# Decoding weights through PSUM, softmax scales moved, and a new order for the prologue

## The chip, the core and the metric

The kernel runs on one core of one Trainium2 chip. A core has five engines that work side by side, each through its own queue in order: TensorE (PE; its weight loads are shown as PEld), VectorE (DVE), ScalarE (ACT), GpSimd (POOL) and SyncE (SP, which here only starts DMAs). They pass work on by semaphores. Tiles lie in SBUF or in PSUM banks of 128 x 512 words, of which this part of the kernel uses eight; TensorE's results go to PSUM, and in this kernel only VectorE and ScalarE read it. [...] The metric is the device time of one execution in microseconds; less is better.

## The reference

```python
q_d = q.reshape(B, H, Sd, 4, D).mean(axis=3)       # also k_d, v_d; B, H, S, D = 4, 8, 576, 64
out_d = sm_attn(q_d, k_d, v_d)                     # softmax(q k^T / 8) v over the pooled sequence
out_up = np.repeat(out_d, 4, axis=2)
mask = np.abs(pos[:, None] - pos[None, :]) < 4     # local attention: 7 keys for each query
scores = np.where(mask, q @ k^T / 8, -1e9)
out_local = softmax(scores) @ v
x = (out_up + out_local) -> 2304 tokens x 512
h = x @ w_in; g = relu(h) ** 2; x = g @ w_out      # d_ff 2048
return ((x @ w_a) * (x @ w_b)) @ w_out2            # d_ff 1536
```

All inputs are fp32, but the host hands the weights over as 64-bit words, and the kernel makes fp32 from the two 32-bit halves itself.

## The kernel before, in words

The tokens are worked in nine tiles of 256. For the first feed-forward network each weight tile (32 of them: 16 of `w_in`, 16 of `w_out`, in the order `w_in` 0, `w_in` 1, `w_out` 0, `w_in` 2, ...) is decoded once, in the prologue, and then kept. A product keeps fp32 accuracy by splitting each operand in a high and a low part and making three passes (`PASSES`), so one hidden block `H` is 12 matmuls of 128x128 by 128x256, and so is one projection `P`.

The prologue is written out by hand as a list of tokens, `ORDER`. Each token issues the instructions of one step, and every engine runs its own in the order of the list; a token's letter says which engine does it (A ScalarE, V VectorE, G GpSimd, S SyncE), a letter a, h, x or y which kind of PSUM bank it takes (three of kind a, three of kind h, one each of x and y; the h kind also serves every `H`, x and y also hold the sums of `P`).

The tokens for a weight n are `wd` (load, `Weight.load`), `wr` (`rescale`, L144), `ws` (`shorten`, L150: the low word to 3 bits), `wa` (`assemble`, L159: two VectorE instructions, L161 and L165, that put the bits together), `wh` (`high`, a rounding copy, L170) and `wl` (`low`, the remainder, L174/L175). All of them work in place in the raw tile in SBUF. A copy goes through the helper `copy` (L125 on ScalarE, L127 or L129 on VectorE and GpSimd).

Tokens with b are the first two tiles' local attention as dense blocks (`Block`: `bs` scores on TensorE, `bm` the mask's addition L483, `bx` the maxima L491 with the scaling L492, `be` exponentials L498, `bd` totals, `bn` normalising, `bt` transposes, `bc` copies, `bw` values, `bo` outputs, `ba` adding the pooled part, `bh` and `bl` the split into high and low, L564). Tokens with p are the pooled attention (`Pooled`: `pa` and `pf` the loads that sum up four positions by DMA, `pj` joining two partial sums L235, `ps` scores L241, `px` maxima L252 with the scaling L253, `pe`, `pd`, `pn`, `pt`, `pc`, `pw`, `po` as above). `H`, `J`, `L`, `P` are the feed-forward steps: hidden matmuls L582, three ScalarE instructions L590 to L593, VectorE's subtraction L596, projection L603. From tile 2 on local attention is done on VectorE and GpSimd (`Local`: L361, L370, L401, L409), planned in events beside the `H` of the tile before. The first of these, one L361 and one L370, come beside H.13 and H.14.

Both lists issue the `H`, `J`, `L` and `P` of tiles 0 and 1 but for the last projections, and after the list a loop goes on with tile 2. The second network (`Pair`, from tile 8 on) decodes its 36 weight tiles with the same `Weight` class in place; it isn't touched.

Of the kernel before, what the change touches and what calls it, by code (L numbers as in the profile page):

```python
# [35 lines left out]
bq.0.S wd.1.A ws.1.A bs.0.1.0.x bs.0.0.1.a bs.0.0.0.a bm.0.0.1 bm.0.0.0 wr.1.V bx.0.0 wa.1 bm.0.1.0 wh.1.V  # L36
bq.1.A wd.0.A pl.0 pa.0.1.0 pa.0.1.1 pf.0.1.2 pf.0.0.2 pa.0.0.0 pf.0.0.3 pa.0.0.1 pf.0.1.3 bs.0.1.1.a wd.2.A
be.0.0 wr.0.A wd.3.S ws.0.A bm.0.1.1 bs.1.1.1.h bm.1.1.1 bx.0.1 bd.0.0 wa.0 wh.0.V wl.0.G wd.6.S wd.4.S wd.5.S
be.0.1 bs.1.0.0.a bs.1.0.1.y bm.1.0.1 bs.1.1.0.y bm.1.0.0 bx.1.0 be.1.0 wr.3.G bd.0.1 bn.0.0.V bm.1.1.0
bt.0.0.0.x bt.0.0.1.y ws.2.A ws.3.A bc.0.0.0.A bd.1.0 bx.1.1 wr.2.A pj.0.0.V bn.1.0.G bn.0.1.G pa.0.1.2  # L40
bt.0.1.0.a wa.2 bt.1.0.0.h bt.0.1.1.a be.1.1 wr.4.G bv.0.S bc.1.0.0.A wr.6.A bc.0.1.0.A pj.0.1.V wh.2.V wl.2.G
bc.0.0.1.V wa.3 wl.1.V bd.1.1 bn.1.1.G wh.3.G wl.3.G ps.0.0.0.a bt.1.0.1.h ps.0.0.1.a ps.0.1.0.a bw.0.0.y
px.0.0.0 ws.4.V px.0.0.1 ws.5.A bc.0.1.1.A ps.0.2.0.a bt.1.1.0.h px.0.1.0 wa.4 bw.0.1.h ps.0.1.1.a pe.0.0.0
pe.0.0.1 pd.0.0 pn.0.0.G bt.1.1.1.h ps.0.3.0.x pt.0.0.1.h wd.9.S bo.0.0.A ws.9.A wr.9.G pa.0.1.3 bc.1.1.0.A
wd.7.S wr.7.A bo.0.1.A bv.1.S wr.5.A bw.1.0.a pt.0.0.0.h wh.4.V bc.1.0.1.V wl.4.V px.0.1.1 wa.5 ws.6.V
pe.0.1.0 wd.8.A pe.0.1.1 wd.10.S pc.0.0.1.A bc.1.1.1.A wh.5.A pd.0.1 ps.0.2.1.h bw.1.1.y ps.0.3.1.h ws.7.A
wa.6 px.0.2.0 pn.0.1.G wl.5.G wd.11.S px.0.2.1 wh.6.A pe.0.2.0 pe.0.2.1 pc.0.0.0.A pw.0.0.a bo.1.0.A bo.1.1.A
wl.6.G wr.10.G px.0.3.0 px.0.3.1 pd.0.2 pn.0.2.V pt.0.2.1.y pt.0.2.0.h pe.0.3.0 wa.7 pe.0.3.1 pd.0.3
pc.0.2.1.A pc.0.2.0.A wh.7.A po.0.0.A ws.8.A pt.0.1.1.h pw.0.2.y pt.0.1.0.x po.0.2.A pc.0.1.0.A wr.8.V ws.11.V
wl.7.V wa.9 wd.13.S pn.0.3.G pc.0.1.1.A wa.8 wr.11.A ws.10.A wa.10 wa.11 wr.13.V wh.9.A wl.9.V wh.8.A  # L50
pt.0.3.1.h pw.0.1.a pt.0.3.0.a pc.0.3.0.A pc.0.3.1.A pw.0.3.h po.0.1.A ws.13.A pl.1 ba.1.0.G ba.0.0.G pa.1.0.0
pa.1.0.1 wd.12.S bh.0.0.A bl.0.0.V wl.8.G wh.11.V wa.13 wh.13.V po.0.3.A ba.0.1.G bh.0.1.A ws.12.A bl.0.1.G
H.0 H.1 H.2 wh.10.A wr.12.A wl.10.G wd.14.S wl.13.G pa.1.0.2 wd.19.A pa.1.1.0 pa.1.1.1 wd.16.S ws.14.A J.0
wa.12 bh.1.0.V ws.19.V L.0 wl.11.V wr.14.A ba.1.1.V wa.14 bl.1.0.G J.1 wh.12.A wr.16.V wd.15.S wd.17.A wl.12.G
wd.18.S wh.14.A ws.15.A ws.16.A P.0 H.3 H.4 bh.1.1.V wr.15.V L.1 wr.19.V wa.16 J.2 J.3 L.2 wa.15 wr.17.V L.3
P.1 wl.14.G wd.20.S bl.1.1.G pa.1.0.3 pa.1.1.2 J.4 ws.17.A wh.16.A P.2 H.5 P.3 H.6 H.7 ps.1.0.0.a wa.17
wr.18.V wl.16.G wh.15.A ws.18.A wr.20.A J.5 wl.15.G wa.18 L.4 wh.17.A wl.17.G wd.23.S wa.19 wd.22.S ws.20.A
wd.21.A L.5 wa.20 P.4 ps.1.0.1.a H.8 H.9 wh.18.A J.6 P.5 L.6 P.6 wr.23.A wh.20.A wr.21.A wh.19.A ws.21.V
px.1.0.0 px.1.0.1 wr.22.A J.7 wa.21 ws.22.V wl.18.G wd.24.S ws.24.V L.7 wh.21.V pe.1.0.0 pe.1.0.1 wl.20.G
pa.1.1.3 wl.19.G J.8 J.9 ps.1.1.0.a P.7 ps.1.2.0.a wl.21.G wr.24.G wd.25.S wa.22 ws.23.V pd.1.0 wh.22.A  # L60
wl.22.G wd.28.S wd.27.S pn.1.0.A pt.1.0.0.a wa.23 wh.23.G px.1.1.0 L.8 wa.24 wr.27.V L.9 wr.25.V wh.24.G
wl.23.G wl.24.G H.10 H.11 P.8 pe.1.1.0 wd.29.A wr.28.A ws.28.A pc.1.0.0.A wd.26.A P.9 ps.1.1.1.a ws.27.A wa.28
ws.25.A wa.25 J.10 J.11 ws.29.A wh.25.A wl.25.G wr.26.A wr.29.A wa.27 L.10 wh.27.A ws.26.A wd.31.A wd.30.S
px.1.1.1 wh.28.V wl.28.G wl.27.G L.11 wa.29 wa.26 H.12 pt.1.0.1.h J.12 wh.29.A wl.29.G wh.26.G wl.26.G L.12
P.10 H.13 pc.1.0.1.A pw.1.0.a wr.31.A po.1.0.A ws.31.A J.13 pe.1.1.1 ws.30.A wr.30.A wa.31 pd.1.1 L.13 wa.30
pn.1.1.G wh.30.G P.11 H.14 J.14 L.14 H.15 wh.31.A J.15 L.15 P.12 P.13 pt.1.1.0.a wl.30.G wl.31.G H.16 J.16
L.16 P.14 P.15 H.17 J.17 L.17 H.18 J.18 P.16.xy H.19 P.17 J.19 L.18 L.19 H.20 J.20 L.20 P.18 P.19 H.21 J.21
H.22 J.22 P.20 H.23 J.23 L.21 P.21 L.22 L.23 H.24 J.24 L.24 H.25 P.22 P.23 J.25 L.25 H.26 J.26 H.27 J.27 L.26
L.27 P.24 P.25 H.28 J.28 H.29 J.29 H.30 J.30 L.28 L.29 P.26 P.27 P.28 H.31 P.29 J.31 L.30 L.31
# [1237 lines left out]
```

## Time and profile before

| | |
|---|---|
| time, median of 3 runs | 971.13 us (970.21 to 972.1) |
| profiled execution | 971.67 us, span 969.9 us, mean granted clock 0.968 |
| PE busy | 911.8 us, 94%, 6128 matmuls |
| DVE busy | 723.0 us, 75%, 974 instructions |
| ACT busy | 500.9 us, 52% |
| POOL busy | 459.5 us, 47% |
| DMA | 161.89 MB, mean 167 GB/s |

Busy shares are averages over stages. Matmuls are pipelined, so a busy PE need not be at its peak. A row of the chain says what the end of the execution was waiting for at that time. In a row of instructions the names are those of the tiles (`raw` is a weight's tile, `w` its split form, `bank` a PSUM bank, `mx` the maxima).

### The profile page before, as it was taken

Reading aid. Unit: us, or ns where it says so; the run is one execution under the profiler, and the core shown is the slowest. Engines: PE = TensorE matmul, PEld = TensorE weight load, DVE = VectorE, ACT = ScalarE, POOL = GpSimd, SP = SyncE. Lnnn points to the kernel's source line nnn. Section 1 sums busy time; section 2 is a strip of 40 time slices with the busy share of each in tenths; the row PEclk is TensorE's granted clock in tenths of the full one; section 3 lists DMA queues with packets and bytes.
Section 4 is the critical chain, followed back from the end, with each engine's and each line's share of the span. In section 5 each row is a group of like instructions: output and inputs, shape, how many; then the busy total and the mean of one; then the engine's idle time right before and its main releaser. Section 6 shows DMA issues by size and latency. Waiting matters only on the chain.

```text
span 969.9 us, 16643 instructions
## 1 busy us (share of the span) xinstructions
PE 911.8 (94%) x6128; PEld 825.0 (85%) x6128; DVE 723.0 (75%) x974; ACT 500.9 (52%) x1274; POOL 459.5 (47%) x388
## 2 busy tenths in 40 slices
...
GB/s 286 234 155 207 228 105 94 101 186 55 99 41 188 113 53 73 63 86 68 46 67 153 104 82 120 261 236 187 235 168 228 212 208 281 404 407 408 259 91 83
DMA packets 69889, 161.89 MB, mean 167 GB/s; under 512 B 8472, under 2 KB 16920, under 8 KB 69808
## 3 DMA queue, kind: packets, MB, share of 16 engines
...
## 4 chain that ended last, share of the span: by engine, by line
PE 72%; DVE 13%; POOL 6%; DMA 3%; issue 3%; ACT 3%; SPq 0%; DVEq 0%; POOLq 0%; ACTq 0%
PE bank L907 34%; PE bank L603 17%; PE bank L582 16%; DVE raw L161 3%; DVE raw L165 2%; POOL pv L410 2%; PE bank L241 2%; POOL pv L409 2%; DVE pv L401 1%; DMA raw<-in_w_in 1%; DMA wo_d<-wos 1%; DVE xb L767 1%; PE bank L304 1%; PE bank L535 1%; DVE raw L155 1%
## 5 line engine op out<-in xcount | busy, mean ns | idle before, releaser
L582 PE MATMUL bank<-xx,w 128*128 128x256 f32 x1728 | 237.8, 289 | 7.8 <-DVE xx L564 4.6
L603 PE MATMUL bank<-g,w 128*128 128x256 f32 x1728 | 237.7, 288 | 6.6 <-DVE g L596 6.6
L907 PE MATMUL bank<-xb,wb 128*128 128x512 f32 x1008 | 232.8, 391 | 6.7 <-ACT r L999 4.8
L582 PEld LDWEIGHTS bank<-xx,w 128*128 128x128 f32 x1728 | 224.0, 198 | 10.3 <-DVE xx L564 5.2
L603 PEld LDWEIGHTS bank<-g,w 128*128 128x128 f32 x1728 | 219.6, 194 | 13.0 <-DVE g L596 7.4
L907 PEld LDWEIGHTS bank<-xb,wb 128*128 128x128 f32 x1008 | 187.9, 188 | 49.5 <-ACT r L999 7.9
L409 POOL TENSOR_TENSOR pv<-pv 128x768 f32<-128x768 f32 x28 | 51.5, 1839 | 170.5 <-DVE pv L401 170.5
L907 PE MATMUL bank<-op,wo 128*128 128x512 f32 (+1 forms) x648 | 131.7, 365 | 0.0
L907 PEld LDWEIGHTS bank<-op,wo 128*128 128x128 f32 x648 | 112.0, 189 | 19.7
L590 ACT ACTIVATE bank<-bank 128x256 f32<-128x256 f32 x144 | 53.1, 369 | 137.4 <-PE bank L582 136.8
L767 POOL TENSOR_TENSOR wb<-raw,wb 128x256 fp32r<-128x256 f32 x96 | 93.5, 995 | 34.3 <-ACT wb L847 30.5
L596 DVE TENSOR_TENSOR g<-bank,g 128x256 fp32r<-128x256 f32 x144 | 59.3, 417 | 63.6 <-ACT g L593 62.8
L401 DVE TENSOR_TENSOR pv<-vt,sc 128x1792 f32<-128x1792 f32 x28 | 82.7, 2954 | 19.5 <-POOL x L412 19.5
L959 POOL TENSOR_TENSOR r<-r 128x512 f32<-128x512 f32 x36 | 54.6, 1516 | 59.3 <-DVE r L956 35.6
L767 DVE TENSOR_TENSOR op<-ys,op 128x512 fp32r<-128x512 f32 x84 | 54.9, 711 | 32.9 <-ACT op L770 32.8
L999 ACT ACTIVATE r<-bank 128x512 f32<-128x512 f32 x72 | 42.8, 595 | 64.2 <-PE bank L907 57.9
L165 DVE SCALAR_TENSOR_TENSOR raw<-raw 128x512 uint32<-128x512 uint32 x68 | 72.5, 1067 | 2.3
L125 ACT ACTIVATE raw<-raw 128x512 uint32<-128x512 uint32 (+1 forms) x113 | 69.8, 670 | 8.6 <-DMA raw<-in_w_in 8.6
L956 DVE TENSOR_TENSOR r<-bank,r 128x512 f32<-128x512 f32 x72 | 48.4, 682 | 29.2 <-PE bank L907 25.4
L161 DVE SCALAR_TENSOR_TENSOR raw<-raw 128x512 uint32<-128x512 uint32 x68 | 60.4, 888 | 10.9 <-ACT raw L125 10.8
L361 DVE TENSOR_TENSOR p<-qt,kt 128x1792 f32<-128x1792 f32 x28 | 61.6, 2198 | 0.0
L410 POOL TENSOR_TENSOR pv<-pv 128x256 f32<-128x256 f32 x28 | 58.9, 2105 | 2.2
...
## 6 DMA issues: line engine op xcount, KB each, us to landing
...
```

The lines of the kernel that those rows point to most:

```text
L125: engine.activation(out=out, in_=in_, func=AF.Copy, scale=scale)
L161: nc.vector.scalar_tensor_tensor(out=low, in0=top, scalar=3, in1=low, op0=ALU.logical_shift_left, op1=ALU.bitwise_or,)
L165: nc.vector.scalar_tensor_tensor(out=low, in0=top, scalar=0x80000000, in1=low, op0=ALU.bitwise_and, op1=ALU.bitwise_or,)
L361: nc.vector.tensor_tensor(out=self.p, in0=q.unsqueeze(2).to_broadcast([P, FACTOR, WIN, D]), in1=window(k), op=ALU.mult,)
L401: nc.vector.tensor_tensor(out=p, in0=window(heads.pop(("v", n))), in1=self.s[:, :, h].unsqueeze(3).to_broadcast([P, FACTOR, WIN, D]), op=A ...
L409: add(out=p[:, :, 0:3], in0=p[:, :, 0:3], in1=p[:, :, 3:6], op=ALU.add)
L410: add(out=p[:, :, 0], in0=p[:, :, 0], in1=p[:, :, 1], op=ALU.add)
L582: nc.tensor.matmul(out=h, lhsT=wi[f].w[:, a, ct * P:(ct + 1) * P], rhs=x_rhs(i, ct, b), start=(n == 0), stop=(n == 3 * NCT - 1),)
L596: nc.vector.tensor_tensor(out=self.g[:, 1], in0=self.h, in1=self.g[:, 0].bitcast(F32), op=ALU.subtract)
L603: nc.tensor.matmul(out=x2[et // 2][:, et % 2 * T1:(et % 2 + 1) * T1], lhsT=wo[f].w[:, a, et * P:(et + 1) * P], rhs=g[:, b], start=(f == 0 ...
L767: engine.tensor_tensor(out=out, in0=in0, in1=in1, op=ALU.subtract)
L907: nc.tensor.matmul(out=out, lhsT=blk[:, a, cols:cols + P], rhs=rhs[b], start=(start and n == 0), stop=(stop and n == 2), skip_group_check= ...
```

## The change

`shorten` can write its result to a PSUM bank (`ws` gets a bank kind; `-` or none means in place, as before), `assemble` then reads it there as one operand and writes its first result there; the second goes back to the raw tile, or stays in the bank (`wa` with `b`). `high` and `low` read wherever it is. The scale of the pooled softmax is put, with its sign, on the pooled queries by a new step `pq`, and the maxima become minima, so that the scaling after the reduction (L253) goes. In the block form the scale goes with its sign into the mask's addition, which becomes a scalar_tensor_tensor, and L492 goes. The mask's sign is turned by the host. `Local` isn't changed. `ORDER` is new as a whole.

```diff
-        def shorten(self, engine):
+        def shorten(self, engine, kind="-"):
             low = self.raw[:, :, 0]
+            self.bits = low if kind == "-" else bank(kind).bitcast(U32)
             if engine is nc.scalar:
-                copy(engine, low, low, 0.9296875 * 2.0 ** -29)
+                copy(engine, self.bits, low, 0.9296875 * 2.0 ** -29)
             else:
                 engine.tensor_scalar(
-                    out=low, in0=low, scalar1=2.0 ** -29, scalar2=7.0, op0=ALU.mult, op1=ALU.min
+                    out=self.bits, in0=low, scalar1=2.0 ** -29, scalar2=7.0, op0=ALU.mult, op1=ALU.min
                 )
-        def assemble(self):
+        def assemble(self, last="-"):
             low, top = self.raw[:, :, 0], self.raw[:, :, 1]
             nc.vector.scalar_tensor_tensor(
-                out=low, in0=top, scalar=3, in1=low,
+                out=self.bits, in0=top, scalar=3, in1=self.bits,
                 op0=ALU.logical_shift_left, op1=ALU.bitwise_or,
             )
+            self.v = low if last == "-" else self.bits
             nc.vector.scalar_tensor_tensor(
-                out=low, in0=top, scalar=0x80000000, in1=low,
+                out=self.v, in0=top, scalar=0x80000000, in1=self.bits,
                 op0=ALU.bitwise_and, op1=ALU.bitwise_or,
             )
...
-            copy(engine, self.w[:, 0], self.raw[:, :, 0].bitcast(F32))
+            copy(engine, self.w[:, 0], self.v.bitcast(F32))
...
-                out=self.w[:, 1], in0=self.raw[:, :, 0].bitcast(F32),
+                out=self.w[:, 1], in0=self.v.bitcast(F32),
...
-            self.steps = []
+            self.steps = [(6, 0, lambda: self.signed(nc.scalar))]
+        def signed(self, engine):
+            copy(engine, self.qd, self.qd, -SCALE / 16)
...
-            nc.vector.tensor_reduce(out=mx, in_=s, axis=AX.X, op=ALU.max)
-            nc.vector.tensor_scalar_mul(out=mx, in0=mx, scalar1=-SCALE / 16)
+            nc.vector.tensor_reduce(out=mx, in_=s, axis=AX.X, op=ALU.min)
...
-                    out=self.a[ct][:, h2, qc], in_=s[:, qc], func=AF.Exp, scale=SCALE / 16,
+                    out=self.a[ct][:, h2, qc], in_=s[:, qc], func=AF.Exp, scale=-1.0,
...
-            nc.vector.tensor_tensor(
-                out=self.p[:, h2, 2 * cp:2 * cp + 2], in0=self.s.pop((h2, cp)),
-                in1=self.band.unsqueeze(1).to_broadcast([P, 2, 2, KB]), op=ALU.add,
+            nc.vector.scalar_tensor_tensor(
+                out=self.p[:, h2, 2 * cp:2 * cp + 2], in0=self.s.pop((h2, cp)), scalar=-SCALE,
+                in1=self.band.unsqueeze(1).to_broadcast([P, 2, 2, KB]), op0=ALU.mult, op1=ALU.add,
...
-            nc.vector.tensor_reduce(out=mx, in_=p, axis=AX.X, op=ALU.max)
-            nc.vector.tensor_scalar_mul(out=mx, in0=mx, scalar1=-SCALE)
+            nc.vector.tensor_reduce(out=mx, in_=p, axis=AX.X, op=ALU.min)
...
-                    out=p[:, n], in_=p[:, n], func=AF.Exp, scale=SCALE, bias=mx[:, n:n + 1],
+                    out=p[:, n], in_=p[:, n], func=AF.Exp, scale=-1.0, bias=mx[:, n:n + 1],
```

Of the new `ORDER`, the lines around J.0 and the end of the weights:

```
bl.0.1.G wh.10.A H.0 wh.13.A H.1 wl.13.G ws.12.V.a wr.12.A wd.14.S wr.14.G wl.10.V J.0 wd.19.A wd.16.S wa.12.b
ws.14.A.a bh.1.0.G L.0 J.1 H.2 pa.1.1.1 wa.14.- wr.16.A bl.1.0.G wh.12.A wl.11.V ba.1.1.V wd.15.S wh.14.A H.3
...
wh.15.A ws.18.V wr.19.V wr.20.A wl.15.V L.4 wh.17.A ws.19.A.a pa.1.1.2 wa.18.- wd.21.S J.5 wd.23.S wl.17.V
wr.21.A ws.20.A.a ps.1.0.1.a wa.19.- L.5 wd.22.A wl.16.G wh.18.G H.8 wr.23.G wa.20 px.1.0.1 wd.24.S P.3 H.9 P.4
...
px.1.1.1 H.12 pc.1.0.1.A J.12 wh.26.A wl.26.G H.13 ws.31.A.h pw.1.0.a wa.31.b pe.1.1.1 L.12 P.11 J.13 po.1.0.V
wr.30.A ws.30.A.h L.13 wa.30 pd.1.1 wl.29.G wh.30.G pn.1.1.A wl.30.G wh.31.A P.12 H.14 J.14 wl.31.V P.13 H.15
```

Counted from the two lists, as before / after; the stretch from H.0 to `wa.30` counts that token too:

| step | before H.0 | H.0 to wa.30 | whole list |
|---|---|---|---|
| `wa`, with a bank behind its `ws` | 0 of 13 / 11 of 13 | 0 of 19 / 15 of 19 | 0 of 32 / 26 of 32 |
| `wa` whose result stays in the bank | 0 / 3 | 0 / 7 | 0 / 10 |
| `ws` on VectorE (into a bank) | 3 / 5 (5) | 5 / 6 (3) | 8 / 11 (8) |
| `ws` on ScalarE (into a bank) | 11 / 8 (6) | 13 / 13 (12) | 24 / 21 (18) |
| `wr` on VectorE, ScalarE, GpSimd | 3, 6, 4 / 7, 2, 4 | 7, 11, 1 / 7, 10, 2 | 10, 17, 5 / 14, 12, 6 |
| `wh` on VectorE, ScalarE, GpSimd | 6, 5, 1 / 4, 8, 0 | 2, 13, 3 / 2, 13, 3 | 8, 19, 5 / 6, 22, 4 |
| `wl` on VectorE, GpSimd | 4, 6 / 5, 5 | 1, 19 / 10, 9 | 5, 27 / 16, 16 |
| `pc`, `po` on VectorE | 0, 0 / 1, 1 | 0, 0 / 1, 1 | 0, 0 / 2, 2 |
| `bc`, `bn`, `pj`, `bh` on VectorE | 2, 1, 2, 0 / 1, 2, 1, 1 | 0, 0, 0, 2 / 0, 0, 0, 1 | 2, 1, 2, 2 / 1, 2, 1, 2 |
| `px`, `bx` | 8, 4 / 8, 4 | 4, 0 / 4, 0 | 12, 4 / 12, 4 |
| `wd`, `pa` | 14, 8 / 14, 10 | 18, 6 / 18, 4 | 32, 14 / 32, 14 |
| `H`, `P` | 0, 0 / 0, 0 | 14, 11 / 14, 12 | 32, 30 / 32, 30 |

## Rows read from the trace of the kernel before

**Rows 1.** The page's chain that ended last, shares of the span by engine.

```profile
PE 72%; DVE 13%; POOL 6%; DMA 3%; issue 3%; ACT 3%; SPq 0%; DVEq 0%; POOLq 0%; ACTq 0%
```

**Rows 2.** The same chain in time: start us, us, what.

```profile
39.44 0.71 PE bank L241 x4
...
59.08 1.97 DVE raw L155
...
196.60 1.44 PE bank L582 x12
```

**Rows 3.** Stretches: us, busy of each engine, PEclk, DMA share, GB/s.

```profile
0.00:20.00 20.00, 6.53 (x112) 5.94 (x112) 5.97 (x15) 5.82 (x20) 3.00 (x9) 1.00 0.92 307
...
40.00:57.00 17.00, 16.55 (x138) 12.99 (x136) 12.78 (x28) 12.23 (x40) 10.41 (x8) 0.51 0.67 198
...
74.00:142.00 68.00, 58.85 (x379) 54.77 (x380) 66.00 (x92) 42.74 (x106) 41.88 (x33) 0.82 0.67 188
142.00:520.00 378.00, 370.82 (x3074) 360.50 (x3073) 287.17 (x351) 180.00 (x529) 166.52 (x127) 1.00 0.34 91
520.00:970.00 450.00, 439.30 (x2291) 376.13 (x2289) 316.59 (x439) 233.70 (x493) 210.28 (x190) 1.00 0.60 218
```

**Rows 4.** Single lines' instructions: duration ns min/median/max, first and last start.

```profile
L161 DVE SCALAR_TENSOR_TENSOR raw<-raw x68: 657/685/1811, 12.5 to 795.7; 128x512 uint32<-128x512 uint32 x68
...
L165 DVE SCALAR_TENSOR_TENSOR raw<-raw x68: 692/1066/1695, 13.2 to 796.4; 128x512 uint32<-128x512 uint32 x68
...
L439 DVE TENSOR_TENSOR xx<-xps,xx x14: 690/691/693, 185.9 to 510.8; 128x512 fp32r<-128x512 f32 x14
...
L956 DVE TENSOR_TENSOR r<-bank,r x72: 671/680/692, 573.4 to 835.3; 128x512 f32<-128x512 f32 x72
...
L767 DVE TENSOR_TENSOR op<-ys,op x84: 677/684/2539, 827.1 to 936.1; 128x512 fp32r<-128x512 f32 x84
...
L127 DVE CAST w<-raw x8: 393/414/426, 14.2 to 127.6; 128x512 fp32r<-128x512 f32 x8
...
L127 DVE COPY aTb<-bank x2: 676/678/679, 33.3 to 42.5; 70x512 f32<-70x512 f32 x2
```

**Rows 5.** VectorE's groups, 74 to 141.6 us: busy, mean ns | idle before.

```profile
L165 DVE SCALAR_TENSOR_TENSOR raw<-raw 128x512 uint32<-128x512 uint32 x20 | 21.8, 1088 | 0.7
L161 DVE SCALAR_TENSOR_TENSOR raw<-raw 128x512 uint32<-128x512 uint32 x20 | 18.6, 930 | 0.1
L155 DVE TENSOR_SCALAR raw<-raw 128x512 uint32<-128x512 uint32 x5 | 6.0, 1219 | 0.0
...
L129 DVE TENSOR_SCALAR raw<-raw 128x512 f32<-128x512 f32 x7 | 5.7, 812 | 0.0
...
L253 DVE TENSOR_SCALAR mx<-mx 72x2 f32<-72x2 f32 x4 | 2.6, 638 | 0.1
```

**Rows 6.** Timeline, two single instructions: start us, us, what.

```profile
39.19 0.17 DVE L253 TENSOR_SCALAR mx<-mx 72x2 f32<-72x2 f32 x1
...
40.66 0.68 ACT L125 ACTIVATE raw<-raw 128x512 uint32<-128x512 uint32 x1
```

**Rows 7.** GpSimd's largest group, 74 to 141.6 us.

```profile
L175 POOL TENSOR_TENSOR w<-raw,w 128x512 fp32r<-128x512 f32 x18 | 27.6, 1541 | 21.6 <-ACT w L125 15.7 <-DVE w L127 5.8
```

**Rows 8.** VectorE's groups, 20 to 74 us.

```profile
L165 DVE SCALAR_TENSOR_TENSOR raw<-raw 128x512 uint32<-128x512 uint32 x11 | 10.9, 990 | 0.4
L161 DVE SCALAR_TENSOR_TENSOR raw<-raw 128x512 uint32<-128x512 uint32 x11 | 10.0, 907 | 3.1 <-ACT raw L125 3.1
L175 DVE TENSOR_TENSOR w<-raw,w 128x512 fp32r<-128x512 f32 x4 | 4.2, 1044 | 0.0
L253 DVE TENSOR_SCALAR mx<-mx 72x2 f32<-72x2 f32 x8 | 4.0, 496 | 0.3
...
L155 DVE TENSOR_SCALAR raw<-raw 128x512 uint32<-128x512 uint32 x3 | 2.8, 935 | 0.0
L564 DVE TENSOR_TENSOR xx<-xb,xx 128x256 fp32r<-128x256 f32 x2 | 2.7, 1387 | 0.0
```

More of the change, by code (lines that the diff above doesn't have):

```diff
@@ L35 @@
 ORDER = """
[L36 to L69, printed above, removed]
+bq.0.S bs.0.0.0.x bs.0.1.0.a wd.1.A bs.0.0.1.a bm.0.0.0 bm.0.0.1 ws.1.A.- pl.0 bq.1.A wd.0.A bm.0.1.0 bs.1.0.1.y
@@ new lines @@
+pa.0.1.0 bx.0.0 pf.0.0.2 bs.0.1.1.a pa.0.0.0 wd.2.A pa.0.1.1 pf.0.1.2 wd.6.S be.0.0 pf.0.0.3 pa.0.0.1 wr.1.V
+wr.0.A bm.1.0.1 bs.1.0.0.y bm.0.1.1 bm.1.0.0 wd.3.S bs.1.1.0.h ws.0.A.h wd.5.S pf.0.1.3 bx.0.1 wa.0.b wh.0.V
+wl.0.V wr.3.G bs.1.1.1.a pj.0.1.G bx.1.0 bd.0.0 be.0.1 bm.1.1.1 bd.0.1 be.1.0 bn.0.1.G wa.1.b bm.1.1.0 bn.0.0.V
+bt.0.0.0.h bd.1.0 wd.4.A pj.0.0.V bt.0.0.1.y wr.2.A bc.0.0.0.A bv.0.S bn.1.0.G bx.1.1 ws.2.V.h bc.0.0.1.V
+bt.1.0.0.x be.1.1 wr.4.G wa.2 pq.0.A bt.0.1.0.a bt.0.1.1.a ws.4.V.h bc.1.0.0.A bc.0.1.0.A ws.3.V.y bc.0.1.1.A
@@ new lines @@
+wa.3 ps.0.0.1.a wh.2.A bd.1.1 ps.0.1.0.a pa.0.1.2 ps.0.0.0.a wl.2.G bn.1.1.V px.0.1.0 bt.1.0.1.h wh.3.A px.0.0.0
+pe.0.0.0 pe.0.1.0 ws.5.V.y wh.1.V bw.0.1.x bw.0.0.h px.0.0.1 bt.1.1.0.a wa.4 pe.0.0.1 bt.1.1.1.h ps.0.1.1.a
+ps.0.2.0.a pd.0.0 wl.1.V wl.3.G pn.0.0.G wh.4.V px.0.1.1 pt.0.0.1.h bo.0.0.A ps.0.3.0.a wr.5.V bc.1.1.0.A wd.7.S
+bv.1.S pa.0.1.3 wr.7.V bo.0.1.A wa.5 wd.9.A pt.0.0.0.h px.0.2.0 px.0.3.0 pe.0.1.1 pd.0.1 bw.1.0.h bc.1.0.1.A
+pc.0.0.1.A bc.1.1.1.A wl.4.G wh.5.A ps.0.2.1.a pc.0.0.0.A wr.9.G bw.1.1.y wr.6.V ps.0.3.1.h wd.8.S wd.10.A
@@ new lines @@
+bo.1.0.A pe.0.3.0 px.0.2.1 ws.6.V.h pe.0.2.0 ws.7.A.h pe.0.2.1 wl.5.V wa.6.b pn.0.1.G wr.10.G pd.0.2 wh.6.A
+pn.0.2.V bo.1.1.A px.0.3.1 wa.7 wd.11.A pw.0.0.a pt.0.2.0.y ws.9.A.- wl.6.V wd.13.A pt.0.2.1.a pt.0.1.0.x
+po.0.0.V pe.0.3.1 pc.0.2.1.A wr.11.V pc.0.2.0.A pw.0.2.y pt.0.1.1.h pd.0.3 wh.7.A wr.8.V po.0.2.A ws.8.A.h
+wl.7.G wa.8 pn.0.3.G pt.0.3.0.a pc.0.1.0.V ws.10.A.a pc.0.1.1.A pw.0.1.a ws.11.A.y ba.0.0.G ba.1.0.G wa.10.b
+pt.0.3.1.x pc.0.3.1.A pc.0.3.0.A wh.8.A pw.0.3.h pl.1 wr.13.V pa.1.0.0 bh.0.0.V wa.11 wd.12.S po.0.1.A wa.9.-
@@ L70 @@
+J.15 L.14 pt.1.1.0.a H.16 J.16 L.15 L.16 H.17 J.17 P.14 P.15 H.18 J.18 H.19 J.19 L.18 L.17 P.16.xy H.20 L.19
+J.20 L.20 P.17 P.18 P.19 H.21 J.21 H.22 J.22 P.20 H.23 J.23 H.24 J.24 L.22 L.21 L.24 P.21 H.25 J.25 L.23 P.22
+H.26 J.26 P.23 L.26 H.27 P.24 J.27 L.25 H.28 L.27 P.25 J.28 H.29 P.26 J.29 H.30 L.29 L.28 P.27 J.30 H.31 J.31
+P.28 L.31 L.30 P.29
 """
```

29 lines of the change are left out of this document (19 added, 10 removed).

## The prediction

> **What bounds the kernel now.** I read the chain that ended last by engine, then in order of time, then the busy time by stretch, then the forms of the instructions that the change touches, then VectorE's and GpSimd's groups in two stretches. In the chain TensorE holds 72% and VectorE 13% [rows 1]; the reader should see that these are two stages. In order of time the chain lies on TensorE for a while from 39.44 us, on VectorE's decoding later (59.08 us and on), and at last on TensorE [rows 2]. By stretch [rows 3] VectorE is busy 66.00 of the 68 us from 74 to 142, TensorE 58.85. From 142 us TensorE is busy 370.82 of 378 and 439.30 of 450 us at clock 1.00, so nothing that another engine saves there can count for much.
>
> So the time is the moment at which the last weight is decoded, about 141.6 us, and a TensorE-bound rest. In both orders that point lies at the same place: 13 weights are assembled before H.0 and 19 from there to `wa.30`; H.0 to H.13 stand before `wa.30`, H.14 after it. Only P.11 moves from behind that point to before it, 12 matmuls, 1.44 us at the upper clock [rows 2], which have to fit into the earlier stage. What counts is how much sooner VectorE gets through its queue to `wa.30`.
>
> **Why VectorE is slow there.** The same instruction has two durations. L161 takes 657 ns at best, 685 in the middle, 1811 at most; L165 692, 1066, 1695 [rows 4]. The forms that stretch have all operands in SBUF: L767's subtracts of that kind go from 677 to 2539 ns. With one operand in PSUM the same width does not stretch: L439 takes 690 to 693 ns over 14, L956 671 to 692 over 72, in stages where GpSimd works as well [rows 4]. After the change 26 of 32 weights have a bank behind `ws` (11 of 13 before H.0, 15 of 19 after), and both assembling instructions of each then read one operand from PSUM: 52 of 64 go over to the class that doesn't stretch.
>
> **The change on VectorE, H.0 to wa.30 (74 to 141.6 us).** Stretch paid now, mean less shortest, by count [rows 4, 5]: L161 20 x (0.930 - 0.68) = 5.0; L165 20 x (1.088 - 0.69) = 8.0; L155 5 x (1.219 - 0.42) = 4.0; L129 7 x (0.812 - 0.42) = 2.7; L253 4 x (0.638 - 0.17) = 1.9, with 0.17 from its bare row [rows 6]; 0.42 is the cast of the same width [rows 4]. Together 21.6 us. The uses that can stretch fall from 58 to about 22 (four weights stay in SBUF, eight instructions; three subtracts from SBUF, three shortenings, seven rescalings, one L361). At the same stretch per use 8.2 us are left; GpSimd is lighter too, with 9 subtracts of L175 in place of the 18 that take 27.6 us [rows 7], by which it would be some 6. I take 7: -14.6.
>
> Against that stands work. VectorE subtracts 10 weights instead of 1: 9 x 0.68 = 6.1. Three of the six shortenings write PSUM: a copy out of a bank takes 676 ns, an SBUF cast of that width 414 [rows 4], so 3 x 0.26, and one more instruction of 0.42, = 1.2. One `pc` and one `po` copy come over (+0.7, each under the 0.68 of a full width), two casts of `bh` and one `pd` go (-0.9), four L253 go (bare -0.7). Sum +6.4. For the PSUM operand of 30 assembling instructions I add 1.0, of 0 to 30 x 0.07 (a bound of a tenth of their 0.69). Stage: -14.6 + 6.4 + 1.0 = -7.2.
>
> [...]
>
> **20 to 74 us.** In the same way [rows 4, 8]: L161 11 x 0.227 = 2.5; L165 11 x 0.30 = 3.3; L175 4 x 0.36 = 1.5; L253 8 x 0.326 = 2.6; L155 3 x 0.515 = 1.5; L564 2 x 0.97 = 1.9, its bare time for 256 columns taken as 0.42: 13.3 us. Uses fall from about 48 to 20, so 5.5 stay. Added: five shortenings into PSUM for three in SBUF, +2.0; four rescalings, +1.3; a subtract, +0.7; two casts less, -0.7; `bh`, `pc`, `po`, `bn` come, `pj` and a `bc` go, +0.5; twelve scalings of maxima go, -1.2: +2.6. PSUM operands +0.6. That is -4.6 on VectorE. From 40 to 57 us, 17 of these 54 us, TensorE is busy 16.55 us at clock 0.51, the lower of its two levels [rows 3], and a shorter VectorE queue gives nothing there: -4.6 x 0.68 = -3.1.
>
> **The scale.** `pq` is one ScalarE copy of 128x576 per batch between `pj` and the first pooled score. ScalarE has room (12.23 of 17 us [rows 3]), but the copy lies on the way of the data; a copy of 128x512 takes 0.68 [rows 6]. If other work stands first on TensorE it costs nothing: +0.4 of 0 to 0.8. `masked` stays one instruction with one operand in PSUM; I take it as unchanged, bounds 0 and 8 x 0.26 (copy less cast, as above). In the main loop batches 2 and 3 lose L253 and get a `pq` each; TensorE's 370.82 of 378 us hide both.
>
> **Other engines and queues.** ScalarE rescales 12 weights for 17, shortens 21 for 24, casts 22 for 19: it falls. GpSimd loses 11 subtracts in all. Before H.0 both orders start 14 weight loads; two more of all go out from ScalarE's queue, and `pa.1.0.2` (GpSimd) and `pa.1.1.0` (SP) go out before H.0; nothing of batch 1 is read before H.7, so this is hidden, and without cover it is two issues. The first 20 us are the DMA's, busy 0.92 [rows 3], with the same bytes in a new order: I put nothing, bounds 2 us either way.
>
> Sum: -7.2 - 3.1 + 0.4 = -9.9 from the execution that gave the rows (971.67 us): 961.8. It lies 0.54 us over the median 971.13; on the median 961.2, and I say 961.
>
> **A new wait.** A shortening into a bank waits for the bank's last reader, often VectorE's `wl` (`ws.19.A.a` stands three tokens behind `wl.15.V`, `ws.20.A.a` two behind `wl.17.V`). It waits in ScalarE's queue; J.5 is queued behind it, and L.5 and P.5 wait for J.5. ScalarE idles 25 of 68 us [rows 3], so I put it at nothing; its bound is the third rival.
>
> **Rivals.**
>
> *TensorE takes over (967).* From 74 to 142 us it is busy 58.85 of 68 us at clock 0.82 [rows 3]. At that clock the stage can give back at most 9.1 us, 7.7 with P.11 moved in; hand-overs leave half, -4. For it: it is that near. Against: 26 H and P at 1.44 [rows 2] are 37.4 us at the upper clock.
>
> *More comes (951).* Denser feeding keeps the upper clock, and 3 and 2 us of stretch remain in place of 7 and 5.5; with nothing lost from 40 to 57 us this is -20.
>
> *Slower, by bank waits (982).* Between a freed bank and `wa` lies a ScalarE shortening of 0.68 us [rows 6]. If VectorE waits this out at each of 26 weights, about 0.8 us with the hand-over, it costs 20.8. From 9.9 / 26 = 0.38 us per weight it eats the gain. For it: three banks of each kind are shared with H and the scores. Against: before, VectorE stood for a shortening only 3.1 us [rows 8], and other work stands between.
>
> *The operand in PSUM doesn't free VectorE (974).* Then only the L253 go (-4.5), the added 9.0 and 1.6 stand: +6.1, with a lighter GpSimd +3. The 72 of L956 speak against.
>
> **How the numbers follow.** Forecast 0.56, own range 955 to 967 (remaining stretch 4 either way, PSUM operand 1.6, the first loads 2); TensorE takes over 0.20; more 0.12; bank waits 0.08; not freed 0.04. With the bounds of the costs, 948 to 969 holds 8 in 10. Within 0.2%, 1.9 us, a measurement of this kernel cannot tell from no change: 0.04, the late end of the TensorE case. Faster 0.56 + 0.16 + 0.12 = 0.84; slower, the last two, 0.12.
>
> **What would show it.** Right: L161's and L165's successors at 0.66 to 0.75 us where they read a bank, their total to `wa.30` near 45 us in place of 62; L253 gone; `wa.30` done near 131 us with H.14 beside it, the rest as before; H.0 some 3 us sooner. Wrong: assembling still near 1 us (not freed); VectorE idle behind ScalarE's shortening (bank waits); VectorE idle while TensorE is full at clock 0.5 (TensorE takes over); or `wa.30` sooner and the span unchanged.

## The result, and the profile after

The changed kernel takes 959.47 us (median of 4 runs, 957.15 to 961.9) against 970.67 us for the kernel before on the same chip; the ratio is 0.988 [0.986, 0.990]. Beside later kernels it took 959.75 us, ratio 0.987 [0.984, 0.990]. The forecast of 961 us missed by 1.5 us, on the faster side. The profiled execution took 957.15 us (span 955.4), the lowest of its four, so about 2 us of its distance to the execution profiled before (971.67 us) belong to that execution.

The page of the changed kernel, the chain's shares and the busy times, answers to [rows 1]:

```profile
PE 71%; DVE 9%; POOL 8%; DMA 6%; issue 3%; ACT 3%; SPq 0%; ACTq 0%; POOLq 0%; DVEq 0%
...
PE 895.9 (94%) x6128; PEld 812.3 (85%) x6128; DVE 699.2 (73%) x957; ACT 498.8 (52%) x1272; POOL 439.2 (46%) x378
```

VectorE's share of the chain falls from 13 to 9%; DMA and GpSimd take part of it. The stretches of the same kernel (us; busy of PE, PEld, DVE, ACT, POOL; PEclk; DMA share; GB/s), beside [rows 3]:

```profile
40.00:57.00 17.00, 11.51 (x163) 9.18 (x159) 15.65 (x30) 12.07 (x44) 8.50 (x7) 0.84 0.84 246
57.00:74.00 17.00, 9.07 (x47) 6.15 (x47) 14.78 (x26) 8.29 (x19) 11.65 (x14) 0.50 0.73 194
74.00:142.00 68.00, 61.15 (x464) 58.02 (x465) 62.60 (x104) 49.27 (x129) 30.47 (x27) 0.94 0.62 188
142.00:520.00 378.00, 373.26 (x3110) 363.57 (x3107) 282.32 (x339) 187.24 (x541) 170.01 (x130) 1.00 0.35 94
```

PEclk is the share of TensorE's full clock that was granted. In windows of 2 us from 20 to 144 us both kernels have it at 0.50 or at 1.00, and between only in windows where it changes: these are the two levels that the forecast speaks of. From 74 to 142 us TensorE now issues 464 matmuls where it issued 379, at granted clock 0.94 instead of 0.82 (the last 13 us of it lie behind `wa.30` now; from 73.11 us to there it is 0.92). VectorE is no longer full, and GpSimd works 30.47 us in place of 41.88.

L161, L165, L155, L175, L129 and L127 of before are L164, L169, L158, L179, L130 and L128 after. The single lines from 20 to 130 us (duration min/median/max in ns), beside [rows 4]:

```profile
L164 DVE SCALAR_TENSOR_TENSOR bank<-raw,bank x26: 678/685/697, 21.9 to 128.0; 128x512 uint32<-128x512 uint32 x26
...
L164 DVE SCALAR_TENSOR_TENSOR raw<-raw x6: 641/682/1507, 26.3 to 120.2; 128x512 uint32<-128x512 uint32 x6
...
L169 DVE SCALAR_TENSOR_TENSOR raw<-raw,bank x16: 687/689/692, 32.6 to 128.7; 128x512 uint32<-128x512 uint32 x16
L169 DVE SCALAR_TENSOR_TENSOR bank<-raw,bank x10: 695/696/697, 22.7 to 126.2; 128x512 uint32<-128x512 uint32 x10
...
L179 DVE TENSOR_TENSOR w<-raw,w x6: 657/706/2948, 42.5 to 101.5; 128x512 fp32r<-128x512 f32 x6
```

Not one of the 52 assembling instructions with an operand in a bank lasts over 0.70 us. The forms that keep all operands in SBUF still stretch: an assembling instruction to 1.51 us, a subtract to 2.95 us.

VectorE's groups from H.0 to `wa.30` (busy, mean ns | idle before), beside [rows 5]:

```profile
L164 DVE SCALAR_TENSOR_TENSOR bank<-raw,bank 128x512 uint32<-128x512 uint32 x15 | 10.3, 688 | 1.0 <-ACT raw L126 0.5 <-POOL raw L130 0.4 <-ACT bank L126 0.2
...
L179 DVE TENSOR_TENSOR w<-raw,w 128x512 fp32r<-128x512 f32 x3 | 5.0, 1658 | 0.0
...
L179 DVE TENSOR_TENSOR w<-bank,w 128x512 fp32r<-128x512 f32 x7 | 4.8, 686 | 3.8 <-ACT w L126 3.8
L130 DVE TENSOR_SCALAR raw<-raw 128x512 f32<-128x512 f32 x7 | 4.4, 644 | 0.8 <-DMA raw<-in_w_in 0.6
```

Two moments cut the execution into three parts: the first unbroken run of H.0's matmuls, and the end of `wa.30`. The timeline after (start, us):

```profile
65.60 0.58 PE L589 MATMUL bank<-xx,w 128*128 128x256 f32 x1
...
73.11 7.87 PE L589 MATMUL bank<-xx,w 128*128 128x256 f32 x41 [0.35 <-POOL xx L571]
...
128.69 0.69 DVE L169 SCALAR_TENSOR_TENSOR raw<-raw,bank 128x512 uint32<-128x512 uint32 x1
```

And before:

```profile
68.17 0.58 PE L582 MATMUL bank<-xx,w 128*128 128x256 f32 x1
...
74.33 5.64 PE L582 MATMUL bank<-xx,w 128*128 128x256 f32 x32 [0.50 <-DVE xx L564]
...
141.00 0.69 DVE L165 SCALAR_TENSOR_TENSOR raw<-raw 128x512 uint32<-128x512 uint32 x1
```

| Part, us | before | after | difference |
|---|---|---|---|
| start to H.0's run | 74.33 | 73.11 | -1.2 |
| H.0's run to the end of `wa.30` | 67.36 | 56.27 | -11.1 |
| `wa.30` to the span's end | 828.2 | 826.0 | -2.2 |

A second profile of the changed kernel (e8, 959.75 us, nearer to the median) has 72.38, 57.78 and 827.84 us in these parts, that is -2.0, -9.6 and -0.4. H.0's very first matmul moves more than its run, from 68.17 to 65.60 us (64.82 in e8), but from there to its run H.0 now takes 7.5 us, before 6.2, waiting for its own input; e4 looks at that.

### The profile page after: what moved, and what is told of

The parts are those of the page before. It is cut to its first block, busy times and chain, and to the rows that moved or that the text cites. A ratio compares the mean times of both kernels' runs of the same rounds, so it can differ in the third digit from the quotient of the medians.

```text
span 955.4 us, 16577 instructions
## 1 busy us (share of the span) xinstructions
PE 895.9 (94%) x6128; PEld 812.3 (85%) x6128; DVE 699.2 (73%) x957; ACT 498.8 (52%) x1272; POOL 439.2 (46%) x378
## 4 chain that ended last, share of the span: by engine, by line
PE 71%; DVE 9%; POOL 8%; DMA 6%; issue 3%; ACT 3%; SPq 0%; ACTq 0%; POOLq 0%; DVEq 0%
PE bank L914 35%; PE bank L610 17%; PE bank L589 16%; DMA raw<-in_w_in 3%; POOL pv L418 2%; DVE pv L409 2%; POOL pv L417 2%; DMA qkd<-in_qk_p 1%; PE bank L250 1%; DVE raw L169 1%; DVE xb L774 1%; PE bank L312 1%; DVE bank L164 1%; DVE w L179 1%; DMA band<-in_mask 1%
## 5 line engine op out<-in xcount | busy, mean ns | idle before, releaser
L610 PE MATMUL bank<-g,w 128*128 128x256 f32 x1728 | 234.2, 286 | 6.6 <-DVE g L603 6.6
L589 PEld LDWEIGHTS bank<-xx,w 128*128 128x128 f32 x1728 | 221.7, 195 | 7.8 <-ACT xx L126 2.9
L610 PEld LDWEIGHTS bank<-g,w 128*128 128x128 f32 x1728 | 216.7, 192 | 12.6 <-DVE g L603 7.4
L777 ACT ACTIVATE op<-ys 128x512 fp32r<-128x512 f32 x84 | 47.1, 624 | 24.3 <-DMA ys<-y_d 13.1
L126 ACT ACTIVATE raw<-raw 128x512 uint32<-128x512 uint32 (+1 forms) x87 | 53.3, 671 | 11.7 <-DMA raw<-in_w_in 9.9
L369 DVE TENSOR_TENSOR p<-qt,kt 128x1792 f32<-128x1792 f32 x28 | 59.1, 2109 | 0.0
L600 ACT ACTIVATE g<-bank 128x256 fp32r<-128x256 f32 x144 | 55.3, 384 | 4.6
L418 POOL TENSOR_TENSOR pv<-pv 128x256 f32<-128x256 f32 x28 | 55.5, 1984 | 2.2
```

The lines of the kernel that those rows point to most:

```text
L126: engine.activation(out=out, in_=in_, func=AF.Copy, scale=scale)
L369: nc.vector.tensor_tensor(out=self.p, in0=q.unsqueeze(2).to_broadcast([P, FACTOR, WIN, D]), in1=window(k), op=ALU.mult,)
L418: add(out=p[:, :, 0], in0=p[:, :, 0], in1=p[:, :, 1], op=ALU.add)
L589: nc.tensor.matmul(out=h, lhsT=wi[f].w[:, a, ct * P:(ct + 1) * P], rhs=x_rhs(i, ct, b), start=(n == 0), stop=(n == 3 * NCT - 1),)
L600: nc.scalar.activation(out=self.g[:, 0], in_=h, func=AF.Copy)
L610: nc.tensor.matmul(out=x2[et // 2][:, et % 2 * T1:(et % 2 + 1) * T1], lhsT=wo[f].w[:, a, et * P:(et + 1) * P], rhs=g[:, b], start=(f == 0 ...
```

## The experiments

The theory: an instruction of VectorE with all operands in SBUF is held up by GpSimd's work, one with an operand in PSUM is not, and the change is worth what this frees. The rivals: the new order does it, the scale part does it, or VectorE's queue was not what held H.0 and `wa.30`. In the blocks below, `+` and `-` lines hold only the tokens that change. Comparisons are ratios to the kernel before, from the same chip; e1, e2, e4 and e6 shared one set of its runs (970.48 us), e3, e7, e10 and e11 another (971.66), the rest a third (971.71). A time of one profile is one execution and lies up to 3.5 us beside its median here (e2).

**e1: the new order without the banks**

```
- wr.0.A ... ws.0.A.h ...       (and so for all 26)
+ wr.0.A ... ws.0.A ...
```

> The new order with every bank letter taken off the shortenings, so all 32 weights are decoded in SBUF again; order, engines and scales stay as after. Theory (an operand in PSUM takes the instruction out of GpSimd's way): the two assembling instructions stretch again, means near 0.85 and 1.0 us where after has 0.69, the subtracts and shortenings on VectorE stretch too, and of the 11 us between 970.7 and 959.5 most is lost: 967 to 976 us. Rival (the new order and the 11 subtracts taken from GpSimd do it, the bank hardly matters): at most 962 us, and the means stay under 0.75.

976.83 us, ratio 1.0055 [1.0033, 1.0076]: slower than before. VectorE's assembling, 20 to 145 us:

```profile
L164 DVE SCALAR_TENSOR_TENSOR raw<-raw 128x512 uint32<-128x512 uint32 x32 | 29.0, 906 | 4.5 <-ACT raw L126 4.3
L169 DVE SCALAR_TENSOR_TENSOR raw<-raw 128x512 uint32<-128x512 uint32 x32 | 27.9, 872 | 1.1
```

The means are back near 0.9 us, 56.9 us in all against 44.9 with the banks. The new order with the scale part, but without the banks, gives nothing; in it the banks are worth 17.4 us.

**e2: banks in the old order, for 19 weights**

```
- ws.0.A  ws.1.A  ws.2.A ...    (9 weights assembled before H.0, 10 after)
+ ws.0.A.a ws.1.A.a ws.2.A.a ...
```

> The old order and the old engines, with a bank behind the shortening of 19 of 32 weights (9 of them before H.0, 10 after) and nothing else: the subtracts stay on GpSimd, the scales as before. Theory: 38 of 64 assembling instructions fall to 0.69 us; they carry 59% of the 18.8 us of stretch, 11 us, part of which passes to the next instruction that needs the way, so 960 to 966 us. Rival (order and lighter GpSimd): 968 to 972 us. Rival (waits for banks): over 972 us.

965.71 us, ratio 0.9946 [0.9918, 0.9973], inside the range. It holds both classes side by side, between the same neighbours (VectorE, 70 to 137 us):

```profile
L167 DVE SCALAR_TENSOR_TENSOR raw<-raw 128x512 uint32<-128x512 uint32 x9 | 10.2, 1133 | 0.3
L162 DVE SCALAR_TENSOR_TENSOR raw<-raw 128x512 uint32<-128x512 uint32 x9 | 8.6, 955 | 0.2
L167 DVE SCALAR_TENSOR_TENSOR raw<-raw,bank 128x512 uint32<-128x512 uint32 x11 | 7.6, 689 | 0.5
L162 DVE SCALAR_TENSOR_TENSOR bank<-raw,bank 128x512 uint32<-128x512 uint32 x11 | 7.5, 686 | 3.6 <-ACT bank L125 2.8 <-ACT raw L125 0.8
```

With a bank 0.69 us, without one 0.96 and 1.13 us, in the same stage. The last column shows the price the forecast feared: VectorE stands 2.8 us, in two waits, for shortenings into a bank. From 20 to 137 us there are three such waits in this order, 5.5 us in all, for 19 weights.

**e6: the kernel before with all 27 of GpSimd's subtracts on VectorE**

```
- wl.0.G ... wl.30.G
+ wl.0.V ... wl.30.V
```

> The kernel before with all 27 of GpSimd's weight subtracts moved to VectorE, nothing through PSUM. It asks whether GpSimd is what stretches VectorE. If so, L161 and L165 come down to means under 0.80 us although both operands stay in SBUF, and the 27 x 0.60 = 16 us that VectorE takes on are about paid by the stretch that goes (33 us from 20 to 142 us, about three quarters of it): 962 to 973 us. If something else stretches them (DMA traffic into SBUF, say), their means stay near 0.92 and 1.05 and the time is 983 to 990 us.

975.02 us, ratio 1.0041 [1.0027, 1.0055]: the time missed its range. The stretch did what was expected. VectorE, 74 to 142 us, beside [rows 5]:

```profile
L165 DVE SCALAR_TENSOR_TENSOR raw<-raw 128x512 uint32<-128x512 uint32 x20 | 14.7, 735 | 0.7
L175 DVE TENSOR_TENSOR w<-raw,w 128x512 fp32r<-128x512 f32 x21 | 14.5, 715 | 4.2 <-ACT w L125 3.5 <-POOL w L127 0.6
L161 DVE SCALAR_TENSOR_TENSOR raw<-raw 128x512 uint32<-128x512 uint32 x20 | 14.4, 718 | 0.0
...
L155 DVE TENSOR_SCALAR raw<-raw 128x512 uint32<-128x512 uint32 x5 | 2.1, 425 | 5.9 <-DMA raw<-in_w_out 3.7 <-DMA raw<-in_w_in 2.2
```

With GpSimd busy 13.5 us of the 68 instead of 41.9, the same two lines of code, still all in SBUF, go from 1.09 and 0.93 us to 0.74 and 0.72. So it is GpSimd's work that stretches them. VectorE is busy 56.9 us there in place of 66.0, and yet `wa.30` ends 1 us later (142.7) and the rest takes 3.8 us longer. The last column says where VectorE's time went: it stands 5.9 us for weights that have not landed and 3.5 us for ScalarE's copies, and in the rest TensorE waits 2.4 us for one of the subtracts, now on VectorE. The list was laid out for subtracts on another engine; one with the loads and copies moved up was not tried.

**e10: banks only for the 15 weights after H.0**

```
- wr.0.A ... ws.0.A.h ...       (and so for the 11 before H.0)
+ wr.0.A ... ws.0.A ...
```

> The changed kernel without the 11 banks of weights before H.0; the 15 after H.0 stay. All banks together were worth 17.4 us in this order (976.8 without them, 959.5 with them). If their worth lies in the stage of the 19 weights after H.0, as the two profiles say (without banks H.0 began 1.75 us later and wa.30 came 15.7 us later), 960 to 963. Rival (worth by count, 11 of 26): 966 to 968.

967.16 us, ratio 0.9955 [0.9942, 0.9968]: the rival's figure. H.0's first matmul of this kernel:

```profile
73.51 0.58 PE L589 MATMUL bank<-xx,w 128*128 128x256 f32 x1
77.43 4.82 PE L589 MATMUL bank<-xx,w 128*128 128x256 f32 x25 [3.35 <-DVE xx L571]
```

It stands 7.9 us later than with all banks (65.60), about the whole loss of 7.7 us. From there to `wa.30` it takes 65.3 us (after 63.8, before 73.5, e1 73.6). So each half of the banks pays in its own stage: the 11 are worth 7.7 us of time and the 15 9.7 us (976.8 - 967.2). How much of the 7.7 is H.0's coming forward is less sure: e1, whose list is the same up to H.0, has its first matmul at 71.46 us, so 6 to 8 us. My expectation, that those before H.0 were worth 2 us, read one profile of e1 against one of the changed kernel, and by a later piece of H.0 (74.86 against 73.11 us) instead of its first matmul.

**e3: the kernel before with the scale part alone**

```
+ pq.0.A behind pj.0.0.V, pq.1.A ahead of ps.1.0.0.a
- nc.vector.tensor_scalar_mul(out=mx, in0=mx, scalar1=-SCALE / 16)
...                              (and the block form, L492, as in the change)
```

> The kernel before, its order kept, with the scale part of the change alone: queries of the pooled attention copied in place times the negative scale, minima for maxima, the factor in the mask's addition, no scalings of maxima. By the forecast's terms VectorE loses 12 scalings before H.0 and 4 after it (2.6 x 0.68 = 1.8 us and 1.9 us), and 0.4 us come for the copy: 967 to 968 against 970.5 for the kernel before. Rival (those scalings lay in VectorE's waits, and the copy on the way of the scores takes back what they give): 970 to 972.

971.28 us, ratio 0.9990 [0.9976, 1.0004]: nothing that can be measured, a miss, and in the rival's range. Where 12 scalings of 6.5 us went, VectorE's assembling grew (20 to 142 us):

```profile
L165 DVE SCALAR_TENSOR_TENSOR raw<-raw 128x512 uint32<-128x512 uint32 x31 | 34.0, 1096 | 1.1
L161 DVE SCALAR_TENSOR_TENSOR raw<-raw 128x512 uint32<-128x512 uint32 x31 | 31.0, 1001 | 5.4 <-ACT raw L125 5.4
```

In the same window before, these 62 took 32.7 and 28.6 us (means 1.053 and 0.922): 3.7 us more now, and 2.3 us more of waiting behind ScalarE's L125. One reading is that the hold-up belongs to GpSimd's instructions, so taking away one SBUF instruction leaves it to the next; no run separates it from the rival's (the scalings lay in VectorE's waits).

**e7: the changed kernel with the scale part undone**

```
- pq.0.A, pq.1.A
+ nc.vector.tensor_scalar_mul(out=mx, in0=mx, scalar1=-SCALE / 16)
...                              (and the block form)
```

> The changed kernel, its order and banks kept, with the scale part undone: the 16 small scalings of maxima come back to VectorE, the two copies go from ScalarE. If VectorE is still what orders the stage, 1 to 3 us more than the changed kernel: 960.5 to 962.5 beside 959.5. Rival (with the banks VectorE has room, and the scale part is worth nothing there): 958.5 to 960.

965.03 us, ratio 0.9932 [0.9915, 0.9949]: 5.5 us over the changed kernel's 959.5, where I expected 1 to 3. H.0's first matmul stands at 71.12 us (65.60 and 64.82 in the two profiles with the scale part), so the loss falls before H.0. The 12 scalings before `wa.30` take 7.2 us (mean 0.604), bare 0.17 each. One of them, half of the sum, on VectorE, and what GpSimd does meanwhile:

```profile
46.52 3.75 DVE L262 TENSOR_SCALAR mx<-mx 72x2 f32<-72x2 f32 x1
```

```profile
46.56 0.85 POOL L233 DMA_DIRECT2D vd<-in_v_p  x1
47.14 1.58 POOL L179 TENSOR_TENSOR w<-raw,w 128x512 fp32r<-128x512 f32 x1
48.41 1.82 POOL L130 TENSOR_SCALAR raw<-raw 128x512 f32<-128x512 f32 x1
```

An instruction on 72x2 elements is recorded with 3.75 us beside them. The same part is worth nothing in the old order (e3) and 5.5 us beside the banks: a likely reason is that the assembling around it can no longer be held up in its place, but that was not tried by itself.

Side by side, an assembling instruction takes 0.69 us with an operand in a bank (e2), up to 1.81 us with all operands in SBUF (L161, kernel before), and in the mean 0.72 to 0.74 us there with GpSimd busy 13.5 of 68 us (e6). By what means GpSimd's work holds up VectorE's, no run shows.

**e4: `pa.1.0.2` moved back behind H.2**

```
- pa.1.0.2 wa.13 ba.0.1.G wl.9.V bh.0.1.A bl.0.1.G wh.10.A H.0 ... pa.1.1.1
+ wa.13 ba.0.1.G wl.9.V bh.0.1.A bl.0.1.G wh.10.A H.0 ... pa.1.1.1 pa.1.0.2
```

In the changed kernel this load of GpSimd's stood for 3.34 us for the previous one into the same tile, with H.0's residual addition (L561) queued behind:

```profile
69.66 0.87 POOL L233 DMA_DIRECT2D qkd<-in_qk_p  x1 [3.34 <-DMA qkd<-in_qk_p]
70.26 1.78 POOL L561 TENSOR_TENSOR xb<-xb,o_sb 128x256 f32<-128x256 f32 x2
```

> The kernel after with one token moved: the third partial sum of batch 1 (pa.1.0.2) goes from before ba.0.1 to behind pa.1.1.1, past H.2. In the trace after, its DMA stands 3.34 us in GpSimd's queue until the sum before it has landed, with the addition ba.0.1 behind it, on which half of H.0 waits. If that is what kept H.0 from coming sooner, H.0's second half starts 2 to 3 us sooner and the time falls by 1 to 3 us under after, 956.5 to 958.5 us. If VectorE's queue is the bound there all the same, H.0 starts sooner and the time stays at 959 to 960 us.

960.46 us, ratio 0.9893 [0.9862, 0.9923]: no gain. GpSimd's wait is gone, but in its profile H.0's run starts at 73.62 us, now with 1.40 us of GpSimd waiting for ScalarE's copy. From H.0's first matmul to its run it takes 5.1 us instead of 7.5, but that first matmul stands at 68.49 us in this profile (963.08 us, the longest of the four). The wait was real, and the times show no gain from taking it away; what held H.0 instead, one profile does not settle.

**e11, e12, e5, e13: more of the same**

```
e11  - wr.17.V wr.18.V wr.19.V wr.24.V wr.27.V wr.28.V wr.29.V   + .A each
e12  - wr.5.V wr.6.V wr.7.V wr.8.V wr.11.V wr.13.V               + .A each
e5   - ws.9.A.- ws.21.V ws.29.V.- wa.14.-   + ws.9.A.h ws.21.V.a ws.29.V.a wa.14.b
e13  all three
```

> The changed kernel with the seven rescalings that VectorE does between H.0 and wa.30 moved to ScalarE: VectorE loses 7 x 0.42 = 2.9 us, ScalarE gains 7 x 0.68 = 4.8 us. If VectorE still sets wa.30 in the changed kernel, 956.5 to 958.5. If the stage is now TensorE's and ScalarE's (VectorE waits some 4 us behind ScalarE's copies there), 959.5 to 963.

> The changed kernel with six rescalings before H.0 (weights 5, 6, 7, 8, 11, 13) moved from VectorE to ScalarE. There they take 0.85 us in the mean on VectorE, all operands in SBUF, where 0.42 is their bare time. If what VectorE does with SBUF operands alone still sets H.0: 2 to 4 us less, 955.5 to 957.5. Rival (ScalarE, in whose queue the copies of H.0's input stand, is late instead): 960 to 964.

> The changed kernel with banks for weights 9, 21 and 29 too, and the result of weight 14 left in its bank for VectorE's subtract. In the changed kernel the assembling that reads only SBUF hardly stretches any more (12 uses, one of 1.51 us, the others at 0.64 to 0.69), so by the theory (a bank frees VectorE from GpSimd's use of SBUF) there is nothing left to win but one subtract of up to 2.9 us: 958 to 960. Rival (a bank is worth some 0.6 us per weight whatever else runs): 956.5 to 957.5.

> The changed kernel with all three edits together: four more banks, and no rescaling on VectorE between the first weight and wa.30. The version meant to beat the changed kernel: 954 to 958 if the terms add, 959 to 963 if ScalarE takes VectorE's place as the engine that is waited for.

| | us | ratio |
|---|---|---|
| e11 | 958.98 | 0.9874 [0.9856, 0.9893] |
| e12 | 961.99 | 0.9887 [0.9864, 0.9910] |
| e5 | 960.43 | 0.9877 [0.9849, 0.9904] |
| e13 | 961.50 | 0.9890 [0.9862, 0.9919] |
| e8, the changed kernel | 959.75 | 0.9869 [0.9841, 0.9896] |

> The changed kernel again, for a closer comparison with the kernels of this set: 959.5, within 0.2%.

None can be told from the changed kernel, so none is a better version. e12 and e13 lie in the ranges that name ScalarE, e11 between its two, e5 0.4 us above its range of no gain. e11 and e12 say what VectorE stands for once ScalarE has more to do. The waits of VectorE (us in total, times, longest) in e11, 20 to 143 us:

```profile
DVE w L179 <- ACT w L126: 5.0, 4, 1.7
DVE bank L164 <- ACT bank L126: 4.1, 4, 2.8
```

and in e12, 20 to 130 us:

```profile
DVE w L179 <- ACT w L126: 6.0, 3, 3.6
DVE mx L261 <- ACT a L271: 5.9, 2, 4.1
```

These three are 3.8, 2.6 and 0.9 us in the changed kernel and 5.6, 2.5 and 0.6 in its second profile (e8), so the wait of the subtracts (L179) says nothing. All waits of VectorE for ScalarE from 20 to 130 us do: 13.7 us in e11 and 17.9 in e12, against 8.0 and 9.4. Moving six rescalings takes VectorE from 46.3 (e8) to 41.1 us of the 54 from 20 to 74 us, and gives no time: it waits for ScalarE instead. e5 agrees with the theory that a bank has no worth of its own. Four more gave nothing: of the 12 assembling instructions that were still in SBUF in the changed kernel, one took 1.51 us and the others 0.64 to 0.69, so that little was left to win.

## Why the prediction was right, and where its terms were off

**Why VectorE was slow.** Right, and shown from both sides: the stretch is gone with an operand in PSUM (0.69 us; changed kernel, e2), nearly gone with GpSimd busy 13.5 of 68 us (0.72 and 0.74; e6), and returns without the banks (0.91 and 0.87; e1). Not every form with its operands in SBUF stretches, though: in the main loop, where L361 goes from 2.01 to 3.08 us, the reduction beside it keeps its length (kernel before; ns, min/median/max):

```profile
L370 DVE TENSOR_REDUCE sc<-p x28: 1987/2009/2019, 141.6 to 472.7; 128x28 f32<-128x1792 f32 x28
```

The assembling totals 44.9 us to `wa.30` (17.8 + 4.9 + 11.0 + 7.0 + 4.2; "near 45" was forecast).

**H.0 to `wa.30`, -7.2 forecast, -11.1 in the profiles (-9.6 by e8's).** Four sizes were off, all on VectorE's queue, as forecast; the mechanism held.
- Stretch left: 7 forecast. Measured by the forecast's bare times: 3 x (1.658 - 0.68) = 2.9 in L179 and 7 x (0.644 - 0.42) = 1.6 in L130, 4.5 us. The term is -17.1, not -14.6.
- Operand in PSUM: 1.0 forecast here and 0.6 before H.0, an estimate of the author's; no run shows such a term. In the changed kernel, from 20 to 130 us, L164 takes 0.685 us in the middle with a bank and 0.682 without, L169 0.689 with one operand in a bank, 0.696 with its result there too and 0.693 without: 0.003 us and less. By the shortest of L164, 0.678 with a bank and 0.641 without, it is at most 0.037.
- Work added: +6.4 forecast. VectorE's busy time in this part falls from 65.36 to 51.43 us, by 13.9; less the 17.1 of stretch that is +3.2. The groups of the two windows say which terms were off. The nine subtracts, the scalings and the small copies came as forecast. But the window before holds 20 assembled weights and the one after 19 (-1.4), two casts of weights are gone besides those of `bh` (-0.8), the one L361 is 0.8 shorter (2.78 to 2.01 us), and two shortenings write a bank in this window instead of three (+0.5 where +1.2 stood). That leaves 2.7 of the 6.4, near the 3.2.
- VectorE's waits: put at nothing, 2.0 us idle before and 4.8 after, +2.8. Of the 4.8, 3.8 are the subtracts that came over, waiting for ScalarE's `w`.

Together -17.1 + 3.2 + 2.8 = -11.1; it closes because the work added is taken as what is left over.

**20 to 74 us, -3.1, and `pq`, +0.4.** By H.0's first matmul -2.6, as forecast (-2.7), by its run -1.2. That the first agrees is partly luck. Up to that matmul VectorE is busy 47.44 us before and 44.82 after, 2.6 less where 4.6 were forecast (43.44 in e8). And the factor 0.68, for a TensorE that is full from 40 to 57 us at clock 0.51, has lost its ground: in the changed kernel TensorE is busy 11.51 of these 17 us at clock 0.84 (row above), and the whole 2.6 come through. "Uses fall from about 48 to 20, so 5.5 stay" holds: 6 x (0.845 - 0.42) in L130, 3 x (0.673 - 0.41) in L128, 2 x (1.074 - 0.68) in L164, 4 x (0.481 - 0.158) in L278 make 5.4. But the account of this part hides two large ones that cancel: without the banks the new order brings H.0 later (71.46 us in e1 against 68.17), and the 11 banks bring it 6 to 8 us sooner (e1, e10).

**"`pa.1.0.2` ... is hidden, and without cover it is two issues."** The step was wrong and cost nothing measurable: the load waited 3.34 us for the previous one to land, with H.0's input queued behind it; with it gone the time stayed (e4).

**The scale.** Its VectorE terms were put at their stretched price in both stages and the sum did not ask whether they add to the rest. They do not: alone they give nothing (e3), beside the banks 5.5 us (e7). That is near the 5.2 that the forecast's terms for them come to (1.9 + 0.7 in one stage, 0.68 of 2.6 + 1.2 in the other), but e7's loss lies before H.0, where the forecast had half of it.

**The rest, 0 forecast.** -2.2 us in these two profiles. That P.11 moved ahead in the list is not the reason: in time, the rest after holds 5380 matmuls and the rest before 5366. The other profiles of this order have 825.6 to 828.6, those of the old one with its subtracts left on GpSimd 829.3 and 830.4 (e3, e2). So some 2 us belong to the order, and a wait of TensorE's in the rest is as large (kernel before; us in total, times, longest):

```profile
PE xps L419 <- POOL x L412: 2.0, 1, 2.0
```

TensorE stands there, at about 190 us, for a sum of the local attention on GpSimd. All four profiles with the old order have this wait of 2.0 us (before, e2, e3, e6), none of the ten with the new order has it.

**The rivals.** *Operand in PSUM doesn't free VectorE* fell with the first rows. *Bank waits* exist, 2.6 us in all (L164 behind ACT bank L126), not 20.8. *TensorE takes over* didn't come: from H.0's run to `wa.30` the clock went from 0.82 to 0.92 with denser matmuls (5.6 and 6.4 per us), as *more comes* supposed, and nothing was lost from 40 to 57 us, as it supposed too; but the added work and the waits stayed. What ate the gain of e11 and e12 is ScalarE's copies in front of VectorE; what bounds the changed kernel as it is they do not show.
